# A load held back by a count of dummy matmuls: who issues three weight tiles, and when

## The chip, the core and the metric

The kernel runs on one core of one Trainium2 chip. A core has TensorE (matmuls and their weight loads), VectorE, ScalarE, GpSimd and SyncE, and sixteen DMA engines that move data between memory and the core. SyncE and ScalarE can both issue DMA transfers, each on a queue of its own. The metric is device time in microseconds (us). The kernel before takes 125.09 us, the median of three runs (124.95 to 125.34).

## The reference

A dense layer, SiLU, and a second dense layer, all in bf16:

```python
B, S, D, F = 1, 2048, 640, 1728
# x: [1, 2048, 640], w1: [640, 1728], w2: [1728, 640]
h = jnp.einsum("bsd,df->bsf", x, w1)
h = jax.nn.silu(h)
out = jnp.einsum("bsf,fd->bsd", h, w2)
```

## The kernel before

The first product is computed transposed: hidden features lie on the partitions, tokens on the free dimension. D is five tiles of 128 ("slabs" of w1, numbered 0 to 4), F is thirteen tiles of 128 and a rest of 64, and the 2048 tokens are four chunks of 512. A matmul takes a 128 x 128 tile of w1 as weights and a 128 x 512 tile of transposed x, and adds into one of eight PSUM banks of 512 columns. x arrives transposed by DMA transposes (`turned`, L89, for chunk 0; L158 for the later chunks), all issued by SyncE.

The first chunk is ordered for the arrival of data. The first eight feature tiles occupy all eight banks. For k = 0 the eight tiles are computed in order (L187 to L191), then sweeps for k = 1, 2, 3 (L192) and a last one for k = 4 that finishes each bank (L194), after which ScalarE applies SiLU (L174). The tile loop for k = 0 waits for the transposed x of tiles 0 and 1 and for the first five weight tiles of slab 0 (`ld_w1[0]`), and at tile 5 for the other three (`ld_w1b`, L190). Each later sweep waits for its slab and its transposed tile of x. The remaining feature tiles of chunk 0, which need two more loads of w1, then chunks 1 to 3, and then the second product follow; there each bank is filled by one group.

The startup is issued as follows. Before the start barrier (`early`, L97) SyncE issues the transpose of tiles 0 and 1 of x (L122), ScalarE the load of tiles 0 to 4 of slab 0 (L123), VectorE writes a small zero tile `z` (L124), and TensorE runs 15 dummy matmuls of 128 x 256 on `z` (`dummies`, L128), whose results are never read. After the barrier SyncE's queue holds, in program order: the load of tiles 5 to 7 of slab 0 (L141), slab 1, slab 2, the transpose of tile 2, slab 3, the transpose of tiles 3 and 4, slab 4, the two remaining parts of w1 (L149, L150), 15 transposes for chunks 1 to 3 and four loads of w2. On ScalarE a table load and a warming activation (L152) come next. `wait` makes an engine wait for a semaphore's value, once per value; `tick` attaches an increment to an instruction. Nothing reorders this at run time: each engine works through its own instructions in the order written, and a wait holds what is behind it on that engine.

All matmuls of the product are recorded under L170, all plain loads and stores under L87, the dummies under L130.

Of the kernel before, what the change touches and what calls it, by code (L numbers as in the profile page):

```python
# [9 lines left out]
def bass_standalone__dense_activation_silu__prompt_kernel(  # L10
# [13 lines left out]
    P = 128  # L24
# [6 lines left out]
    HB = 256  # L31
# [6 lines left out]
    pe, act, dve, pool, sp = nc.tensor, nc.scalar, nc.vector, nc.gpsimd, nc.sync  # L38

    with ExitStack() as es:  # L40
        def sb(name, shape, dtype):
            return es.enter_context(nc.sbuf_tensor(name, shape, dtype))
# [10 lines left out]
        z = sb("z", [P, 2], bf16)  # L53
        ps = es.enter_context(nc.psum_tensor("ps", [P, NB, BANK], fp32))
# [4 lines left out]
        def sem(name):  # L59
            s = es.enter_context(nc.semaphore(name))  # L60
            count[s.name if hasattr(s, "name") else name] = 0
            return [s, 0]

        def tick(ins, s, n=1):
            ins.then_inc(s[0], n)
            s[1] += n
            return (s, s[1])

        def wait(eng, *points):
            for pt in points:  # L70
                if pt is None:
                    continue
                s, v = pt
                key = (id(eng), id(s))
                if seen.get(key, 0) < v:
                    eng.wait_ge(s[0], v)
                    seen[key] = v

        s_pe, s_act, s_dve = sem("s_pe"), sem("s_act"), sem("s_dve")
# [4 lines left out]
        def load(eng, out_ap, in_ap):  # L84
            s = sem(f"s_ld{n_dma[0]}")
            n_dma[0] += 1
            return tick(eng.dma_start(out=out_ap, in_=in_ap), s, 16)  # L87

        def turned(c0, c1, k0, k1):  # L89
            s = sem(f"s_tr{n_dma[0]}")  # L90
            n_dma[0] += 1
            return tick(sp.dma_start_transpose(
                out=xT[:, k0:k1, c0:c1], in_=xf[c0:c1, k0 * P:k1 * P]), s, 16)
# [3 lines left out]
        def early(emit, engine, arrived=True):  # L97
            n = len(nc.main_func.blocks[0].instructions)
            r = emit()
            lst = nc.main_func.blocks[0].instructions  # L100
            new = lst[n:]
            del lst[n:]
            at = next(
                i for i, ins in enumerate(lst)
                if ins.opcode == ("EventSemaphore" if arrived else "Drain") and ins.engine == engine
            )
            lst[at:at] = new
            return r
# [3 lines left out]

        NO = NB
        NA = 5
        CO = NO * P

        def slab(eng, k, f0=0, f1=NO):
            return load(eng, w1s[:, k, f0 * P:f1 * P], w1_v[:, k, f0 * P:f1 * P])
# [3 lines left out]
        ld_t[0] = ld_t[1] = early(lambda: turned(0, SCH, 0, 2), ET.SP)  # L122
        ld_w1[0] = early(lambda: slab(act, 0, 0, NA), ET.Activation)  # L123
        p_z = early(lambda: tick(dve.memset(z[:, :], 0.0), s_dve), ET.DVE, False)  # L124

        bank_free = [None] * NB

        def dummies(n):  # L128
            for _ in range(n):
                pe.matmul(ps[:, 3, 0:HB], lhsT=z[:, 0:1].broadcast_to([P, P]),  # L130
                          rhs=z[:, 0:1].broadcast_to([P, HB]), start=True, stop=True)

        def first_dummies():
            wait(pe, p_z)
            dummies(15)

        early(first_dummies, ET.PE)

        p_warm = tick(pool.memset(warm[:, :], 0.0), s_pool)  # L139

        ld_w1b = slab(sp, 0, NA, NO)  # L141
        ld_w1[1] = slab(sp, 1)
        ld_w1[2] = slab(sp, 2)
        ld_t[2] = turned(0, SCH, 2, 3)
        ld_w1[3] = slab(sp, 3)
        ld_t[3] = ld_t[4] = turned(0, SCH, 3, DT)
        ld_w1[4] = slab(sp, 4)
        CM = CO + 2 * P
        ld_rest = load(sp, w1s[:, :, CO:CM], w1_v[:, :, CO:CM])  # L149
        ld_rest2 = load(sp, w1s[:, :, CM:F], w1_v[:, :, CM:F])  # L150
# [37 lines left out]
        for ft in range(NO):  # L188
            if ft == NA:
                wait(pe, ld_w1b)  # L190
# [209 lines left out]
```

## Time and profile before

| what | value |
|---|---|
| median of three runs | 125.09 us (124.95 to 125.34) |
| the profiled execution's own time | 124.8 us |
| its span, first to last instruction | 123.2 us |
| TensorE busy | 120.9 us (98%) |
| ScalarE busy | 38.8 us (31%) |
| granted TensorE clock | 1.0 |
| DMA moved | 10.38 MB |

In the lines of the profile, PE is TensorE, PEld its weight loads, ACT ScalarE, DVE VectorE, SPq and ACTq the DMA issues of SyncE and ScalarE. A timeline line gives start and duration in us, engine, source line, operation, what is written from what, the count, and in brackets the idle time of that engine ahead of it with what ended it. A line of the chain that ended last gives start, duration and what. A line by stretch gives the window, its length, busy time of TensorE, its weight loads, VectorE, ScalarE and GpSimd, the granted clock, the share of time that the sixteen DMA engines had packets in flight, and GB/s. The landing of a transfer is when the last of its sixteen semaphore increments is recorded.

### The profile page before, as it was taken

Reading aid. Unit: us, or ns where it says so; the run is one execution under the profiler, and the core shown is the slowest. Engines: PE = TensorE matmul, PEld = TensorE weight load, DVE = VectorE, ACT = ScalarE, POOL = GpSimd, SP = SyncE. Lnnn points to the kernel's source line nnn. Section 1 sums busy time; section 2 is a strip of 40 time slices with the busy share of each in tenths; the row PEclk is TensorE's granted clock in tenths of the full one; section 3 lists DMA queues with packets and bytes.
Section 4 is the critical chain, followed back from the end, with each engine's and each line's share of the span. In section 5 each row is a group of like instructions: output and inputs, shape, how many; then the busy total and the mean of one; then the engine's idle time right before and its main releaser. Section 6 shows DMA issues by size and latency. Waiting matters only on the chain.

```text
span 123.2 us, 1779 instructions
## 1 busy us (share of the span) xinstructions
PE 120.9 (98%) x797; PEld 55.5 (45%) x797; DVE 6.8 (6%) x11; ACT 38.8 (31%) x67; POOL 0.3 (0%) x5
## 2 busy tenths in 40 slices
PE   8999999999999999999999999999999999999993
PEld 6344444444444444444444444444444444444452
DVE  0000000000000000000000022002201300222001
ACT  4002975555555555555530011001101200110110
POOL 1000000000000000000000000000000000000000
PEclk9999999999999999999999999999999999999999
DMA  6999845445990000000000004202200220022122
GB/s 141 238 255 306 162 112 94 97 93 101 345 366 10 0 5 0 3 0 0 0 0 5 0 13 113 50 0 106 106 0 5 106 106 0 5 106 106 53 74 86
DMA packets 19479, 10.38 MB, mean 84 GB/s; under 512 B 13456, under 2 KB 18960, under 8 KB 19472
## 3 DMA queue, kind: packets, MB, share of 16 engines
q1 hardware_dynamic: 19184, 10.05, 31.1%
q10 hardware_dynamic: 288, 0.23, 0.7%
q8 instruction: 6, 0.10, 0.3%
q14 instruction: 1, 0.01, 0.0%
HBM read 4.51 MB, written 2.62 MB: 58 GB/s over the span
## 4 chain that ended last, share of the span: by engine, by line
PE 94%; DMA 3%; ACT 0%; issue 0%
PE ps L170 94%; DMA w1s<-in_w_dram 3%; ACT o_sb L244 0%
## 5 line engine op out<-in xcount | busy, mean ns | idle before, releaser
L170 PE MATMUL ps<-xT,w1s 128*128 128x512 bf16 (+1 forms) x280 | 59.1, 381 | 0.1
L170 PE MATMUL ps<-w2s,hT 64*128 64x512 bf16 (+3 forms) x377 | 46.2, 369 | 0.0
L170 PEld LDWEIGHTS ps<-xT,w1s 128*128 128x128 bf16 (+1 forms) x280 | 26.4, 99 | 32.7 <-DMA w1s<-in_w_dram 0.8
L174 ACT ACTIVATE hT<-ps 128x512 bf16<-128x512 f32 x52 | 30.0, 608 | 28.9 <-PE ps L170 28.9
L170 PEld LDWEIGHTS ps<-w2s,hT 64*128 64x128 bf16 (+1 forms) x377 | 21.0, 95 | 24.2 <-issue 0.2
L244 ACT CAST o_sb<-ps 128x512 bf16<-128x512 f32 (+1 forms) x9 | 4.9, 550 | 41.5 <-PE ps L170 41.5
L170 PE MATMUL ps<-hT,w2s 64*128 64x512 bf16 x104 | 11.7, 376 | 0.0
L170 PEld LDWEIGHTS ps<-hT,w2s 64*128 64x128 bf16 x104 | 5.0, 94 | 6.3 <-issue 0.4
L242 DVE CAST o_sb<-ps 128x512 bf16<-128x512 f32 (+1 forms) x8 | 5.4, 675 | 40.5 <-PE ps L170 40.5
L242 DVE CAST oT<-ps 128x512 bf16<-128x512 f32 x2 | 1.4, 692 | 73.7 <-PE ps L170 73.7
L244 ACT CAST oT<-ps 128x512 bf16<-128x512 f32 x2 | 1.2, 585 | 10.6 <-PE ps L170 10.6
L130 PE MATMUL ps<-z 128*128 128x256 bf16 x15 | 3.4, 419 | 0.4 <-DVE z L124 0.4
L170 PE MATMUL ps<-w2t,hTt 64*128 64x512 bf16 (+2 forms) x17 | 2.9, 363 | 0.0
L130 PEld LDWEIGHTS ps<-z 128*128 128x128 bf16 x15 | 2.1, 147 | 1.2 <-DVE z L124 0.4
L174 ACT ACTIVATE hTt<-ps 128x512 bf16<-128x512 f32 x2 | 1.2, 597 | 1.1 <-PE ps L170 1.1
L152 ACT ACT_TABLE_LOAD x1 | 1.3, 1283 | 0.7 <-PEq L385 0.7
L170 PEld LDWEIGHTS ps<-w2t,hTt 64*128 64x128 bf16 x17 | 0.9, 94 | 1.1
L170 PE MATMUL ps<-hTt,w2t 64*128 64x512 bf16 x4 | 0.8, 376 | 0.0
L170 PEld LDWEIGHTS ps<-hTt,w2t 64*128 64x128 bf16 x4 | 0.2, 94 | 0.2
L152 ACT ACTIVATE warm<-warm 128x32 f32<-128x32 f32 x1 | 0.2, 229 | 0.0
L139 POOL MEMSET warm<- 128x32 f32 x1 | 0.1, 124 | 0.3 <-POOLq L385 0.3
L385 POOL MEMSET const-bfloat16-1.0<- 128x1 bf16 x1 | 0.1, 101 | 0.0
(4 smaller groups left out, 0.4 us busy)
## 6 DMA issues: line engine op xcount, KB each, us to landing
out_dram<-o_sb SPq DMA_DIRECT2D x15, 160.0 KB, 1.8
w2s<-in_w_dram SPq DMA_DIRECT2D x1, 1120.0 KB, 6.4
w1s<-in_w_dram SPq DMA_DIRECT2D x4, 256.0 KB, 3.9
w2s<-in_w_dram SPq DMA_DIRECT2D x1, 960.0 KB, 8.6
w1s<-in_w_dram SPq DMA_DIRECT2D x1, 560.0 KB, 6.4
w1s<-in_w_dram SPq DMA_DIRECT2D x1, 320.0 KB, 5.2
xT<-in_x_dram SPq DMA_TRANSPOSE x18, 3.7
w1s<-in_w_dram ACTq DMA_DIRECT2D x1, 160.0 KB, 2.5
```

Of the source, the lines that this page charges most:

```text
L130: pe.matmul(ps[:, 3, 0:HB], lhsT=z[:, 0:1].broadcast_to([P, P]), rhs=z[:, 0:1].broadcast_to([P, HB]), start=True, stop=True)
L139: p_warm = tick(pool.memset(warm[:, :], 0.0), s_pool)
L152: act.activation(out=warm[:, :], in_=warm[:, :], func=ACT.Silu)
L170: return pe.matmul(o, lhsT=l, rhs=r, start=start, stop=stop, skip_group_check=shared)
L174: r = tick(act.activation(out=out_ap, in_=in_ap, func=ACT.Silu), s_act)
L242: r = tick(dve.tensor_copy(out=out_ap, in_=in_ap), s_dve)
L244: r = tick(act.copy(out=out_ap, in_=in_ap), s_act)
L385: nc = _bacc.Bacc("TRN2", target_bir_lowering=False, num_devices=1)
```

## The change

The load of tiles 5 to 7 of slab 0 is issued by ScalarE instead of SyncE. ScalarE first waits until the tenth dummy matmul has ended. SyncE issues slabs 1 and 2 as before and then waits for the end of the twelfth dummy before it issues the transpose of tile 2. To make these waits possible, the tenth and the twelfth dummy increment TensorE's semaphore.

```diff
         NO = NB
         NA = 5
+        HELD = (9, 11)
...
+        ticks = {}
+
         def dummies(n):
-            for _ in range(n):
-                pe.matmul(ps[:, 3, 0:HB], lhsT=z[:, 0:1].broadcast_to([P, P]),
+            for i in range(n):
+                ticks[i] = pe.matmul(ps[:, 3, 0:HB], lhsT=z[:, 0:1].broadcast_to([P, P]),
                           rhs=z[:, 0:1].broadcast_to([P, HB]), start=True, stop=True)
 
         def first_dummies():
             wait(pe, p_z)
             dummies(15)
+            for i in HELD:
+                ticks[i] = tick(ticks[i], s_pe)
...
-        ld_w1b = slab(sp, 0, NA, NO)
+        wait(act, ticks[HELD[0]])
+        ld_w1b = slab(act, 0, NA, NO)
         ld_w1[1] = slab(sp, 1)
         ld_w1[2] = slab(sp, 2)
+        wait(sp, ticks[HELD[1]])
         ld_t[2] = turned(0, SCH, 2, 3)
```

## Prediction

> **What bounds the kernel now.** I read the page from the top: engine shares, the chain that ended last, then the timeline of the first 12 us, and last the landing records of the transfers that the first matmuls wait for.
>
> ```profile
> span 123.2 us, 1779 instructions
> ...
> PE 120.9 (98%) x797; PEld 55.5 (45%) x797; DVE 6.8 (6%) x11; ACT 38.8 (31%) x67; POOL 0.3 (0%) x5
> ...
> PE 94%; DMA 3%; ACT 0%; issue 0%
> PE ps L170 94%; DMA w1s<-in_w_dram 3%; ACT o_sb L244 0%
> ...
> w1s<-in_w_dram ACTq DMA_DIRECT2D x1, 160.0 KB, 2.5
> ```
>
> TensorE is busy 98% of the span and makes 94% of the chain; the remaining 3% is one load of w1. The chain in order of time says which:
>
> ```profile
> 1.50 0.06 issue
> 1.56 3.70 DMA w1s<-in_w_dram
> 5.26 0.05 issue
> 5.31 116.03 PE ps L170 x776
> ```
>
> The load issued at 1.56 us is the one that the change moves: tiles 5 to 7 of slab 0 (96 KB), first of SyncE's plain loads. It lands at 5.26, TensorE starts tile 5 at 5.31, and from there to 121.33 nothing interrupts it. So the change can only act before 5.3 us, or by making a later transfer late. The timeline there:
>
> ```profile
> 0.09 1.34 SPq L92 DMA_TRANSPOSE xT<-in_x_dram  x1
> 0.21 0.37 ACTq L87 DMA_DIRECT2D w1s<-in_w_dram  x1
> 0.38 3.38 PE L130 MATMUL ps<-z 128*128 128x256 bf16 x15 [0.38 <-DVE z L124]
> 0.73 1.28 ACT L152 ACT_TABLE_LOAD   x1 [0.73 <-PEq L385]
> 1.56 1.43 SPq L87 DMA_DIRECT2D w1s<-in_w_dram  x3
> 3.04 1.16 SPq L92 DMA_TRANSPOSE xT<-in_x_dram  x1
> 3.65 0.13 PEld L170 LDWEIGHTS ps<-xT,w1s 128*128 128x128 bf16 x2 [0.37 <-DMA xT<-in_x_dram]
> 5.30 0.33 PEld L170 LDWEIGHTS ps<-xT,w1s 128*128 128x128 bf16 x3 [0.55 <-DMA w1s<-in_w_dram]
> 5.90 20.02 PEld L170 LDWEIGHTS ps<-xT,w1s 128*128 128x128 bf16 x94 [0.27 <-DMA w1s<-in_w_dram]
> ```
>
> The reader is to see four things. The dummies end 0.1 us before the transposed x of tiles 0 and 1 arrives (landing 3.61, start 3.65); the change touches neither. Tile 4 starts at 4.871 and the pace is 0.216 us, so tile 5 could have started at 5.087 and started at 5.306: TensorE lost 0.22 us there, not the 0.55 that the weight load's idle time shows, since loads run ahead of matmuls. At 5.90 the weight load waited for slab 1 (landed 5.86), but the matmul started at 5.964, on the pace: slab 1 was just in time. And 0.22 us is all that is left to win by loads after 3.65, 0.18% of the time.
>
> ```profile
> 2.00:3.00 1.00, 1.00 (x7) 0.69 (x6) 0.00 (x0) 0.24 (x2) 0.00 (x0) 1.00 1.23 265
> 3.00:4.00 1.00, 1.00 (x5) 0.35 (x4) 0.00 (x0) 0.00 (x0) 0.00 (x0) 1.00 0.93 98
> 4.00:5.00 1.00, 1.00 (x5) 0.35 (x3) 0.00 (x0) 0.00 (x0) 0.00 (x0) 1.00 0.77 281
> 5.00:6.00 1.00, 0.94 (x6) 0.31 (x5) 0.00 (x0) 0.00 (x0) 0.00 (x0) 1.00 1.23 329
> ```
>
> By stretch (the last two columns are the DMA share and GB/s), the transfer engines are nearly full from 2 us on. From 3 to 4 us they are occupied but move only 98 GB/s: the first 768-byte packets of the moved load took 0.3 to 1.27 us each on most engines, against 0.036 once running. That is why it needs 3.70 us, and one straggling engine set 5.26 (half had landed by 4.47).
>
> **The change part by part.** *ScalarE issues the load.* The tenth dummy starts at 2.276; its modelled time is 0.42, and a semaphore event follows a modelled end by 0.01, so the wait ends at 2.71. ScalarE's last store was issued 0.03 after the event it waited for, so the issue is at 2.74, 1.18 later than now. Its landing is not shown, so I bound it. Below: that store, 64 KB, took 1.55 from issue to landing, giving 4.29 and no wait at all, a gain of 0.22 and no more. Above: the load's own 3.70, giving 6.44 and tile 5 at 6.49, a loss of 6.49 - 5.31 = 1.18. Between: the load of tiles 0 to 4 by the same engine from the same rows, 160 KB, issued 0.21, landed 2.67: 2.47. That is the nearest row (same queue, same source, with transposes in flight beside it). Its packets took 0.055 and the smaller ones take 0.036, eight on each engine, so 0.15 less: 2.32, which gives 5.06. I add 0.04 for packets of slabs 1 and 2 between them, an estimate and my weakest one: 5.10, tile 5 at 5.15, idle 0.06 instead of 0.22. Gain 0.16.
>
> [...] The trace shows 0.084 for a running 2048-byte packet. [...]
>
> *What is queued behind the wait on ScalarE:* the activation table load (1.28) and the warming activation (0.23). They move from 0.73 to about 3.1 and end near 4.7; the first real activation is at 11.56. Cost 0, covered by 6.8 us.
>
> *SyncE without that load.* Slabs 1 and 2 are issued at about 1.56 and 2.05 instead of 2.11 and 2.57. Slab 1 is due next: with tile 5 at 5.15 its first matmul is due at 5.80, and by its old landing it would start at 5.90 and give back 0.10 of the gain. It now has no 96 KB ahead of it, 0.29 of packets on each engine, so I take 5.57 and cost 0; the bounds are 0 and 0.10.
>
> *SyncE's wait.* The twelfth dummy starts at 2.702, so its event is at 3.14 and the transpose is issued at 3.16 instead of 3.04. Everything behind it on SyncE's queue moves by 0.12: slab 3, the transpose of tiles 3 and 4, slab 4, both remaining w1 loads, fifteen transposes of later chunks, the w2 loads. Their slack, due time less landing: transpose of tile 2, 7.69 - 7.17 = 0.52; tiles 3 and 4, 9.42 - 9.02 = 0.40; slab 4, 11.15 - 10.87 = 0.28; the next w1 load, 12.87 - 11.99 = 0.88; chunk 1, 18.3 - 16.8 = 1.5. With TensorE 0.16 earlier and SyncE 0.12 later slab 4 is left with nothing, and all others with some. Cost 0, with bounds of 0 (the transfer engines are backed up, so a later issue need not land later) and 0.12. If the earlier slabs did land sooner, nothing is gained, since TensorE does not idle after 5.3.
>
> *The two semaphore increments on dummies and two waits* add no matmul: 0.
>
> **Sum.** -0.16 on the profiled 124.8 us (span 123.2 and 1.6 around it): 124.64. That execution is 0.29 under the median of the timed runs, 125.09, whose forecast is 124.93, say 124.9.
>
> **The rivals.**
> *The load comes late (slower).* Place: tile 5. The stalled first packets speak for it: if an engine is held until 4.54, as one was, and then moves the load's eight packets (0.036 each) among eight of a slab's (0.084 each), they take 0.96, and with 0.36 from last packet to landing (the row of ScalarE's store) the load lands near 5.86, tile 5 at 5.91, a loss of 0.60: 125.7. Against it: the same bytes now wait behind the stall on one queue, and may pass on the other. The change turns into a loss once it lands after 5.26, and counts as slower from 5.64. The bound is 1.18: 126.3.
>
> *A larger gain.* The timed runs lie up to 0.54 above the profiled one. If that is a longer stall of this same load, removing it brings them near 124.8 - 0.22 = 124.6, or 0.5 under the median. For it: one engine's 1.27 us packet set the landing, which is a matter of chance. Against: nothing in one execution shows where the others lose time.
>
> *Hidden or given back.* Slab 1 or slab 4 takes up the gain, or the load lands at 5.26 again: 125.1.
>
> **How the numbers follow.** A measurement of this kernel tells about 0.3%, 0.38 us, from no change. Forecast (load in time, 0.05 to 0.22 won): 0.33. Given back, or a loss within 0.38: 0.18. Late by more than that: 0.28. Larger gain: 0.21. A fifth of the forecast's cases (0.07) pass 0.3% because the medians themselves spread by that much, and a quarter of the larger gains (0.05) fall short of it: faster 0.07 + 0.16 = 0.23, slower 0.28, same the remaining 0.49. The likeliest case alone reaches from 124.75 to 125.05. The range takes in the larger gain at 124.5 and the late load up to 125.75, leaving out a still later landing.
>
> **What would show it.** In the changed profile: ScalarE's second load issued near 2.74 and landing within 2.4 us; the weight load of tile 5 before 5.1 us; its matmul 0.216 to 0.3 after that of tile 4; the transpose of tile 2 issued near 3.16; no idle time of TensorE at sweeps 1 to 4. I am wrong if the chain of waits still names a load of w1 that ends after 5.26, if it names slab 1 or slab 4, or if the clock row or the start at 3.65 moves, for which I see no reason.

## The result

The changed kernel takes 126.04 us in the median of six runs (125.93 to 126.35), the kernel before 125.11 us in the median of six: ratio 1.008, 95% interval 1.0061 to 1.0099. It is slower by 0.8%, above the range of the forecast. The profiled execution took 125.93 us with a span of 124.4, against 124.8 and 123.2 before. (One ratio below, that of ScalarE's wait alone, rests on two of its four executions, since the granted clock fell in the other two.)

The page of the changed kernel: its span, its engine shares and the chain that ended last, by engine and by line.

```profile
span 124.4 us, 1779 instructions
...
PE 121.4 (98%) x797; PEld 55.7 (45%) x797; DVE 6.8 (5%) x11; ACT 38.8 (31%) x67; POOL 0.3 (0%) x5
...
PE 95%; DMA 3%; issue 0%; ACT 0%; DVE 0%
PE ps L177 93%; DMA w1s<-in_w_dram 3%; PE ps L133 2%; ACT o_sb L251 0%; DVE z L125 0%
```

The shares say almost nothing: 98% busy both times. What is new is that dummies (L133) stand in the chain. In order of time (start, duration, what):

```profile
0.38 2.33 PE ps L133 x10
2.71 0.02 issue
2.73 3.66 DMA w1s<-in_w_dram
6.39 0.05 issue
6.43 116.03 PE ps L177 x776
```

Ten dummies, then the moved load, then TensorE without a break. The last piece is 116.03 us with 776 instructions, exactly as before; it starts at 6.43 instead of 5.31. That is 1.12 of the 1.13 us between the two profiled executions, so everything happens ahead of tile 5. The load is issued 1.17 later and takes nearly as long as it did: 3.66 against 3.70. The timeline up to there:

```profile
1.55 0.96 SPq L87 DMA_DIRECT2D w1s<-in_w_dram  x2
3.10 1.28 ACT L159 ACT_TABLE_LOAD   x1 [3.10 <-PE ps L133]
3.15 1.15 SPq L92 DMA_TRANSPOSE xT<-in_x_dram  x1
3.69 0.13 PEld L177 LDWEIGHTS ps<-xT,w1s 128*128 128x128 bf16 x2 [0.41 <-DMA xT<-in_x_dram]
4.10 0.15 PEld L177 LDWEIGHTS ps<-xT,w1s 128*128 128x128 bf16 x1 [0.28 <-issue]
4.53 0.15 PEld L177 LDWEIGHTS ps<-xT,w1s 128*128 128x128 bf16 x1 [0.28 <-issue]
4.96 0.15 PEld L177 LDWEIGHTS ps<-xT,w1s 128*128 128x128 bf16 x1 [0.27 <-issue]
6.43 19.54 PEld L177 LDWEIGHTS ps<-xT,w1s 128*128 128x128 bf16 x92 [1.32 <-DMA w1s<-in_w_dram]
6.43 19.81 PE L177 MATMUL ps<-xT,w1s 128*128 128x512 bf16 x91 [0.67 <-DMA w1s<-in_w_dram]
```

Slabs 1 and 2 go out first (1.55), and TensorE, with tiles 0 to 4 done, waits for tiles 5 to 7. Slab 1 has by then long landed (5.38); it used to land after the load. One more thing is to be seen: the weight loads of tiles 2 to 4 stand 0.43 apart, twice the 0.216 of the later matmuls. TensorE was still at half pace in this execution until 5.38, where before it reached full pace at 4.44. The long wait hides that here: the matmuls of tiles 0 to 4 end later than they did, and the wait for the load covers it. TensorE's own idle time is the 0.67 of the matmul row; the 1.32 is that of the weight loads, which run ahead of the matmuls (tile 4: 4.96 and 5.38).

The DMA records show where the load was. Its first packet on any transfer engine starts at 4.77, 2.04 us after the issue; before, the first started 1.35 after it. On each engine the eight packets then follow each other 0.033 apart. None of them takes more than 0.036, so nothing stalls them once they are up; they are simply late. The last of the sixteen engines starts its eight at 5.69. What stalled before has moved to slab 1: its first packets, from 2.93 on, took up to 1.27 us where 0.084 is usual for 2048 bytes. After the packets comes one more delay. The load's increments are recorded behind its packets between 5.03 and 5.96, but land only between 6.21 and 6.39; before, they were recorded from 3.77 to 4.93 and landed from 4.09 to 5.26.

### The profile page after: what moved, and what is told of

It is laid out like the page before. It is cut to its first block, busy times and chain, and to the rows that moved or that the text cites. A ratio compares the mean times of both kernels' runs of the same rounds, so it can differ in the third digit from the quotient of the medians.

```text
span 124.4 us, 1779 instructions
## 1 busy us (share of the span) xinstructions
PE 121.4 (98%) x797; PEld 55.7 (45%) x797; DVE 6.8 (5%) x11; ACT 38.8 (31%) x67; POOL 0.3 (0%) x5
## 4 chain that ended last, share of the span: by engine, by line
PE 95%; DMA 3%; issue 0%; ACT 0%; DVE 0%
PE ps L177 93%; DMA w1s<-in_w_dram 3%; PE ps L133 2%; ACT o_sb L251 0%; DVE z L125 0%
## 5 line engine op out<-in xcount | busy, mean ns | idle before, releaser
L133 PE MATMUL ps<-z 128*128 128x256 bf16 x15 | 3.4, 419 | 0.4 <-DVE z L125 0.4
L133 PEld LDWEIGHTS ps<-z 128*128 128x128 bf16 x15 | 2.1, 146 | 1.2 <-DVE z L125 0.4
```

The costliest lines, as they stand in the source:

```text
L133: ticks[i] = pe.matmul(ps[:, 3, 0:HB], lhsT=z[:, 0:1].broadcast_to([P, P]), rhs=z[:, 0:1].broadcast_to([P, HB]), start=True, stop=True)
```

## The experiments

**The theories.** *Order:* each transfer engine works through packets in the order in which they were queued, on whichever queue; the loss is the 512 KB of slabs 1 and 2 that now lie ahead of the load. Rivals: *the queue* (ScalarE's transfers are served behind SyncE's); *issue time* (1.17 us later, whatever lies ahead); *the later transposes* (SyncE's wait); a *fixed delay* of the first plain packets after a transpose.

Each kernel below left one profiled execution. Landings are of the load of tiles 5 to 7: the ninth and the last of its sixteen increments, in us. "Queued ahead" counts slabs and later transposes issued before the load, on either queue; the first transpose is ahead of it in every row.

```
kernel                              queued ahead       issued  ninth  last   tile 5   ratio (95%)
before                              -                  1.56    4.47   5.26   5.31     1
SyncE's wait alone                  -                  1.55    4.25   4.75   4.80     1.0016 (0.9983-1.0049)
ScalarE, no waits                   -                  0.73    3.76   4.01   5.31     1.0016 (0.9989-1.0043)
ScalarE after the 3rd dummy         -                  1.24    3.87   5.60   5.64     1.0012 (0.9987-1.0037)
ScalarE after the 6th dummy         slab 1             1.88    5.43   6.15   6.19     1.0018 (0.999-1.0046)
slab 2 behind SyncE's wait          slab 1             2.73    4.83   6.36   6.41     1.006  (1.0032-1.0089)
changed, slabs 1 and 2 halved       2 halves           2.73    4.81   5.55   5.59     1.0017 (0.9993-1.004)
changed                             slabs 1, 2         2.73    6.31   6.39   6.43     1.008  (1.0061-1.0099)
changed, again                      slabs 1, 2         2.73    6.10   6.18   6.22     1.0048 (1.0023-1.0074)
order alone, all on SyncE           slabs 1, 2         2.57    6.07   6.13   6.18     1.0069 (1.0044-1.0094)
ScalarE's wait alone                slabs, transpose   2.73    7.21   7.48   7.52     1.012  (1.0053-1.0187)
```

**Order alone.** Nothing on ScalarE and no wait; SyncE issues the load third.

```diff
-        ld_w1b = slab(sp, 0, NA, NO)
         ld_w1[1] = slab(sp, 1)
         ld_w1[2] = slab(sp, 2)
+        ld_w1b = slab(sp, 0, NA, NO)
```

> No waits and nothing on ScalarE: SyncE issues slab 1, slab 2, then the load of tiles 5 to 7 (near 2.6 us). Order theory: nearly the whole loss is here, the load lands at 6.2 to 6.5, tile 5 starts near 6.4, time 126.0, ratio 1.007. Rival, the queue (transfers on ScalarE's queue are served after SyncE's): on SyncE's own queue the loss goes, landing near 5.3 to 5.6, time 125.1 to 125.4.

Measured: 125.67 us (125.50 to 126.23), ratio 1.0069. The chain of this kernel, in order of time:

```profile
2.52 0.05 issue
2.56 3.57 DMA w1s<-in_w_dram
6.13 0.05 issue
6.18 116.03 PE ps L170 x776
```

The same picture with another queue and without a dummy in it: the load lands at 6.13, a little ahead of the 6.2 to 6.5 expected. This nearly reproduces the loss; the queue falls as its cause.

**SyncE's wait alone.** The load first on SyncE, as before; only the wait ahead of the transpose of tile 2 is kept.

```diff
         ld_w1b = slab(sp, 0, NA, NO)
         ld_w1[1] = slab(sp, 1)
         ld_w1[2] = slab(sp, 2)
+        wait(sp, ticks[HELD[1]])
```

> The load of tiles 5 to 7 stays first on SyncE; only SyncE's wait for the twelfth dummy ahead of the transpose of tile 2 is kept. Order theory (each transfer engine works through its packets in the order in which they were queued, so the loss is that slabs 1 and 2 now lie ahead of the load): the load lands near 5.3 us as in the kernel before, time 125.1, ratio 1.000. Rival, the later transposes (they now collide with the load or push the rest back): the load lands later than 5.6 or a later sweep idles, time 125.5 or more.

Measured: 125.0 us, ratio 1.0016 with 1 inside the interval; the load lands at 4.75, half a microsecond before the 5.3 expected, and no sweep waits in the profile beyond an idle 0.15 at tile 5. The wait costs nothing that can be measured.

**ScalarE's wait alone.** The changed kernel without SyncE's wait.

```diff
-        wait(sp, ticks[HELD[1]])
```

> The changed kernel without SyncE's wait: the transpose of tile 2 is issued near 2.5 us. Order theory: the load still lies behind slabs 1 and 2 and lands at 6.2 to 6.6, time 126.0, ratio 1.007; a few tenths more if the transpose's packets also come ahead of it. Rival, the later transposes: without that wait the loss goes, time 125.1.

Measured: 126.39 and 126.44 us in two executions, 128.58 and 128.63 in the other two; ratio 1.012 by the first two. The rival expected the loss to go with this wait and is refuted: it stays. Whether it grew is not shown by the times, since the interval (1.0053 to 1.0187) overlaps that of the changed kernel. The transpose of tile 2 now goes out at 2.57, ahead of the load, and in the profile, which is of the execution at 128.63, the load lands at 7.48, 1.09 later than in the changed kernel and later than any theory gave. The two shorter executions have no profile. Their spans of 124.8 and 124.9 put tile 5 near 6.9, an estimate that takes everything from tile 5 on from the changed kernel: some 0.5 later than there. So without SyncE's wait one more transfer gets ahead, and the load lands some 0.5 to 1.1 later. By stretch (window, length, busy time and count of TensorE, weight loads, VectorE, ScalarE, GpSimd, granted clock, DMA share, GB/s):

```profile
5.00:6.00 1.00, 0.04 (x1) 0.00 (x0) 0.00 (x0) 0.00 (x0) 0.00 (x0) 1.00 1.16 217
6.00:7.00 1.00, 0.00 (x0) 0.00 (x0) 0.00 (x0) 0.00 (x0) 0.00 (x0) 1.00 1.18 223
7.00:8.00 1.00, 0.48 (x2) 0.20 (x3) 0.00 (x0) 0.00 (x0) 0.00 (x0) 0.71 1.10 257
8.00:9.00 1.00, 1.00 (x4) 0.38 (x3) 0.00 (x0) 0.00 (x0) 0.00 (x0) 0.50 1.19 299
```

TensorE is idle from about 5.0 to 7.52; at 7.41 the clock row falls to 0.50 and stays there for 3.41 us. In this execution TensorE then took 117.64 us from tile 5 on, where the changed kernel took 116.03: 1.61 more, the other price of the long wait if the idle time brought the clock down, which no run tests alone.

**The load early on ScalarE.** No waits; ScalarE issues it straight after the start barrier.

```diff
-        ld_w1b = slab(sp, 0, NA, NO)
+        ld_w1b = slab(act, 0, NA, NO)
```

> ScalarE issues the load straight after the start barrier, near 0.7 us, with no wait on a dummy and none on SyncE. Order theory: its packets come ahead of slabs 1 and 2, it lands before 4.5 and tile 5 starts on the pace; but 96 KB more lie beside the first transpose, which may push the first matmul from 3.65 to 3.65 to 3.95. Time 124.8 to 125.2. Rival, the queue: it lands after slabs 1 and 2 here too, near 6, time 126.

Measured: 125.08 us, ratio 1.0016, no change. Timeline:

```profile
0.21 0.89 ACTq L87 DMA_DIRECT2D w1s<-in_w_dram  x2
2.56 1.15 SPq L92 DMA_TRANSPOSE xT<-in_x_dram  x1
3.75 0.58 SPq L87 DMA_DIRECT2D w1s<-in_w_dram  x1
4.22 1.84 PEld L170 LDWEIGHTS ps<-xT,w1s 128*128 128x128 bf16 x10 [0.93 <-DMA xT<-in_x_dram]
```

On ScalarE's queue the load lands at 4.01, so that queue was not served last here. But the first transpose lands at 4.17 instead of 3.61 and the first matmul starts at 4.22 instead of 3.65, later than the 3.95 allowed for: the wait has moved from the weights to x. From there TensorE runs at full pace without a break, and tile 5 starts at 5.31, when it started before.

**After the third and the sixth dummy.** The changed kernel with one number changed; for the sixth dummy it is `(5, 11)`.

```diff
-        HELD = (9, 11)
+        HELD = (2, 11)
```

> The changed kernel with ScalarE's wait on the third dummy: the load is issued near 1.24 us, ahead of slabs 1 and 2, behind most of the first transpose. Order theory: no slab ahead, landing 4.0 to 5.2, tile 5 on the pace or 0.2 late, first matmul 3.65 to 4.2 as far as its packets push the transpose; ratio 0.998 to 1.002. Issue-time theory: landing near 4.9, ratio 0.999.

> The changed kernel with ScalarE's wait on the sixth dummy instead of the tenth: the load is issued near 1.88 us, after slab 1 (1.55) and before slab 2 (2.1). Order theory, by arrival across both queues: one slab ahead, landing 5.5 to 5.9, ratio 1.003 to 1.005, as with slab 2 held back although it is issued 0.85 earlier. Issue-time theory: the landing moves with the issue, 5.5. If instead the two queues take turns, the load lands by 5.0 and the ratio is 0.999.

Measured: 125.07 us, ratio 1.0012, and 125.22 us, ratio 1.0018; neither differs from the kernel before. With no slab ahead the ninth increment comes at 3.87, with slab 1 ahead at 5.43. The last increments, 5.60 and 6.15, are set by a few engines and fall outside the bounds given for them; the time with one slab ahead is better than the 1.003 to 1.005 expected. The profiled execution of the latter took 125.68, the longest of its ten (from 124.97), so its landing is no typical one.

The packets of the sixth-dummy run contradict the order theory in its strict form. The load is issued at 1.88, 0.33 after slab 1 and 0.2 before slab 2. The records name a packet's queue but not its engine; the engine is read here from the spacing. At the end of this load, packets of 768 bytes on ScalarE's queue start at 5.10, 5.21, 5.32, 5.44 and 5.55, 0.113 apart, and 0.033 after each of the first four a packet of 2048 bytes of SyncE's queue starts (0.113 is 0.033 and 0.080, the pace of the two sizes). So here the packets of the two queues alternate on an engine, one by one. In this run most of the load's packets stand so, and after the third dummy those on a few engines. In the changed kernel, its repetition and the one with half the slabs, each engine's eight packets stand in one run, 0.033 apart, with no turn among them.

**One slab ahead.** The changed kernel with slab 2 issued after SyncE's wait.

```diff
         ld_w1[1] = slab(sp, 1)
-        ld_w1[2] = slab(sp, 2)
         wait(sp, ticks[HELD[1]])
+        ld_w1[2] = slab(sp, 2)
```

> The changed kernel with slab 2 moved behind SyncE's wait for the twelfth dummy, so that only slab 1 is queued ahead of the load of tiles 5 to 7, which ScalarE still issues near 2.73 us. Order theory: eight packets of 2048 bytes fewer ahead on each engine, 0.65 us; the load lands at 5.6 to 5.9 instead of 6.39, time near 125.5, ratio 1.003 to 1.005. Issue-time theory (the load is late because ScalarE issues it 1.18 us later, whatever lies ahead): it lands near 6.4 as in the changed kernel, ratio 1.008.

Measured: 125.89 us (125.12 to 126.14), ratio 1.006: above the order theory's 1.003 to 1.005, though the interval (1.0032 to 1.0089) reaches into it. Thirteen increments have landed by 4.99, but three land only at 6.33 to 6.36. On three engines the load's packets took turns with those of slab 2, although that was issued 0.42 after it: they start 0.113 apart there and end between 5.48 and 5.70, where the other engines are done by 4.65. Why it was these three, and why they landed another 0.7 after their last packet, is not shown. The ninth increments (4.83 here, 6.31 in the changed kernel) overstate the difference, since 6.31 contains the late landing described above. The run is also not clean: slab 2 is issued at 3.15 instead of 2.11, and everything behind it 0.38 later than in the changed kernel, so the time can't be put down to the load alone. Inconclusive as to size.

**Half the slabs, and the changed kernel again.** The clean test of the amount: same order, same waits, same issue times, half the bytes ahead. The kernel with half the slabs leaves out part of the product.

```diff
-        ld_w1[1] = slab(sp, 1)
-        ld_w1[2] = slab(sp, 2)
+        ld_w1[1] = slab(sp, 1, 0, 4)
+        ld_w1[2] = slab(sp, 2, 0, 4)
...
+        def wt(k, ft):
+            f = ft - 4 if k in (1, 2) and 4 <= ft < 8 else ft
+            return w1s[:, k, f * P:(f + 1) * P]
```

> The changed kernel, same order, same waits, but slabs 1 and 2 are loaded only for tiles 0 to 3 (128 KB instead of 256 KB each); wherever tiles 4 to 7 of these two slabs are used, the weights of tiles 0 to 3 stand in, so that part of the product is left out. Only the amount queued ahead of the load of tiles 5 to 7 changes. Order theory: sixteen packets on each engine of 1024 instead of 2048 bytes, about 0.04 us less each, 0.64 in all: the load lands at 5.6 to 5.9 instead of 6.39, time 125.3 to 125.5, ratio 1.003 to 1.004. Rival, a fixed delay (start-up of the first plain packets after the transpose, or the ScalarE queue itself): it lands at 6.2 to 6.5 and the ratio stays at 1.007 to 1.008.

> The changed kernel once more, for a comparison on the same chip: the load lands at 6.2 to 6.6, time near 126.0, ratio 1.006 to 1.010. Every theory expects this; under the order theory the half of the engines land within 0.3 us of the last, since all carry the same packets ahead.

Both ran on one chip. Changed again: 125.69 us, ratio 1.0048, under the 1.006 to 1.010 expected. Half the slabs: 125.07 us, ratio 1.0017, no change from the kernel before and better than the 1.003 to 1.004 expected. The chains, first the changed kernel again, then with half the slabs:

```profile
2.73 3.45 DMA w1s<-in_w_dram
6.18 0.05 issue
```

```profile
2.73 2.82 DMA w1s<-in_w_dram
5.54 0.05 issue
```

Issued at the same moment on the same queue, the load takes 0.63 us less when 256 KB less lie ahead, and the medians of the times differ by 0.62. Issue time alone would have given no difference, a fixed delay neither. That 0.63 is so near the 0.64 reckoned from the packets is partly luck: the load's packets end 0.73 to 0.79 earlier (first, ninth and last engine), and a longer way from the last packet to the landing, 0.58 against 0.42, takes some of it back. So the bytes of the slabs ahead are shown as the cause of the late load; that packets are always served in the order of issue is not.

**Six tiles first.** The kernel before with one tile more in ScalarE's first load, an attempt at a version that beats both.

```diff
-        NA = 5
+        NA = 6
```

> The kernel before with six tiles of slab 0 in ScalarE's first load instead of five, and two tiles in the load that SyncE issues. From the row of five tiles (0.055 a packet), 0.1 us more beside the first transpose: first matmul 3.65 to 3.75; the second load is 64 KB and is due one matmul (0.216) later, so the idle time of 0.22 goes: ratio 0.998 to 1.000. If the first transpose is pushed back by as much as with the load issued at 0.7 us (0.6), ratio 1.002 to 1.004.

Measured: 124.84 us against 124.97, ratio 0.9994 (0.9966 to 1.0021). The idle time at tile 5 goes, and the time does not. Its weight loads say why:

```profile
3.67 0.13 PEld L170 LDWEIGHTS ps<-xT,w1s 128*128 128x128 bf16 x2 [0.39 <-DMA xT<-in_x_dram]
4.08 0.15 PEld L170 LDWEIGHTS ps<-xT,w1s 128*128 128x128 bf16 x1 [0.28 <-issue]
4.50 0.15 PEld L170 LDWEIGHTS ps<-xT,w1s 128*128 128x128 bf16 x1 [0.28 <-issue]
4.93 0.15 PEld L170 LDWEIGHTS ps<-xT,w1s 128*128 128x128 bf16 x1 [0.28 <-issue]
5.36 3.63 PEld L170 LDWEIGHTS ps<-xT,w1s 128*128 128x128 bf16 x17 [0.28 <-issue]
```

No load of w1 is waited for, but TensorE is at half pace until 5.36. No kernel here beats the one before by more than the measurement tells.

## Why the prediction was wrong

*The failed step* is the landing of the load, in "ScalarE issues the load", and in it the 0.04 "for packets of slabs 1 and 2 between them". Issue at 2.74 was right (2.73). The landing was forecast 2.36 us after it and came 3.66 after it, at 6.39 instead of 5.10. The load's first packet started 2.04 after the issue, with both slabs through on its engine, where the first packet of ScalarE's first load had started 1.01 after its issue (0.21, 1.21). Half of the slabs measured 0.63 where all of them were priced at 0.04. Whether the 2.32 under that term was right is open, since no run issues the load at 2.73 with no slab ahead. Taking another 0.63 off the 2.82 of the run with half the slabs gives 2.19, an estimate, and that is near it. The row of the first load was near in queue and source and far in the one thing that counts, since no slab lay ahead of it.

*Turns between the queues*, which the 0.04 supposes, did not come in the changed kernel. No run shows that term; what the runs showed in its place is the load's packets on each engine in one run of eight behind both slabs, and the landing at 6.39. But turns do occur: after the sixth dummy single packets of 768 and of 2048 bytes alternate at the end of the load, 0.113 from one pair to the next. Why there are none in the changed kernel, where the load was issued 0.62 after slab 2, is not shown. Which engine issued the load behind both slabs made no difference that the ratios can tell apart: 1.0069 on SyncE, 1.008 and 1.0048 on ScalarE.

*The rival that came true* is the late load, with the right place (tile 5) and a price of 0.60 where 1.12 was measured. Its mechanism is half right. Packets do stall, but those of slab 1, and the engines are again occupied and move little from 3 to 4 us (share 0.80, 115 GB/s):

```profile
3.00:4.00 1.00, 1.00 (x5) 0.35 (x4) 0.00 (x0) 0.90 (x1) 0.00 (x0) 1.00 0.80 115
```

The load's own packets neither stall nor move among a slab's; they come behind both slabs, and that made the difference to 0.60. The rival's upper bound, the load's old 3.70 us after the new issue, gave 6.44, near the measured 6.39. That is luck: the 3.70 were 1.35 to the first packet, then packets with stalls among them until 4.93, and the 3.66 are 2.04 to the first packet and none stalled. With fewer or more bytes ahead the load took from 2.82 to 4.75 after the same issue.

*What was right.* The table load and the activation moved from 0.73 and 2.02 to 3.10 and 4.40, behind the wait, and cost nothing. Slab 1 was relieved: 5.38, where 5.57 was taken. SyncE's transpose went out at 3.15 (3.16), and no later sweep waited: from 6.43 on TensorE ran the same 116.03. That the wait costs nothing that can be measured was shown by the run that keeps it alone; what it is good for, keeping the transpose behind the load, the prediction did not see.

*What was not priced.* The larger gain was put down to a longer stall of the load in the timed runs. The profiles offer something else: the moment at which TensorE reaches full pace differs between executions, from 3.08 (SyncE's wait alone, whose last two dummies start 0.113 apart instead of 0.213) to 6.03 (slab 2 behind SyncE's wait). Four or five matmuls at 0.427 instead of 0.216 are up to a microsecond, about the spread of the kernel before on these chips (124.19 to 125.52). That this makes the spread was not tested by a run of its own. It would also say why the 0.22 of idle time was no sure gain, as the run with six tiles first suggests: where TensorE starts slow, tile 5 is due later and the load can be in time anyway.

## What to carry to other kernels

Before a load is moved, count the bytes that will be queued ahead of it on the transfer engines, over all queues; a place behind half a megabyte instead of ahead of it made tile 5 start 0.87 to 1.12 us later here, whichever engine issued the load. Do not count on turns between the queues to bring it forward: they are seen in some of these runs, and in the changed kernel they are not. A row that is near in kind (queue, size, source) but had no such bytes ahead of it is no bound for one that has. And a wait that looks idle may be what keeps another transfer behind the one that matters: without it the load landed later here, by 1.09 in the profile.

## What was not expected of the hardware

Two queues were served in two ways. In the changed kernel the load's first packet started 2.04 us after its issue, and on each engine only behind the slabs' last packets, though it stood on another queue. After the sixth dummy, with the load issued between the slabs, most of its packets alternated with theirs, the last five 0.113 apart. What decides between the two is open.

A load is not there when its packets are through. In the changed kernel the first increment is recorded at 5.03 and the first lands at 6.21, 1.18 later; in the kernel before the same distance is 0.32. What held them is not shown.

In the profiled execution with ScalarE's wait alone, TensorE sat idle for 2.49 us ahead of tile 5, and the granted clock fell at the end of that stretch: 1.0 from 4.00 to 7.41, 0.5 from 7.41 to 10.83. With the order alone it sat idle for 1.35 us at the same place, and the clock stayed at 1.0. That the length of the idle stretch makes the difference is not shown.

With the dummies starting at 0.38 in every profile, full pace came between 2.7 us (SyncE's wait alone, 3.08) and 5.65 us (slab 2 behind SyncE's wait, 6.03) after the first of them. What sets the moment is not shown.

Single transfer engines were more than a microsecond behind the others here: 1.37 between the thirteenth and the last with one slab ahead, 1.73 between the ninth and the last after the third dummy. The tail, not the middle, set the start of the matmul: after the third dummy the ninth increment landed at 3.87, the last at 5.60, and tile 5 started at 5.64. With one slab ahead the tail is the engines on which the queues took turns.
